# A replanned order, shared PSUM banks, and the bonus term added by VectorE after four SBUF transfers, in a linear-attention and MLP kernel

## The chip, the cores and the metric

The kernel runs on one core of one Trainium2 chip. The metric is the device time of one execution in microseconds (us). One profiled execution gives the trace; its times are counted from the start of its span. TensorE is PE in the profile (PEld is its weight load), VectorE is DVE, ScalarE is ACT, GpSimd is POOL, and SyncE is SP, which issues all DMAs here.

## The reference

The input is `r, k, v, w` of 4 batches, 8 heads, 768 tokens and 48 values a head, and `u` of 8 heads by 48. The attention is a recurrence over the tokens; its output is then, token by token, the input of an MLP.

```python
for t in range(S):
    cur = np.einsum('bhd,bhe->bhde', u[None] * kt, vt)
    y[:, :, t] = np.einsum('bhd,bhde->bhe', rt, state + cur)
    state = wt[:, :, :, None] * state + np.einsum('bhd,bhe->bhde', kt, vt)
...
h = x @ w_in            # x: 3072 x 384, w_in: 384 x 2048
g = np.maximum(h, 0.0) ** 2
return g @ w_out        # w_out: 2048 x 384
```

The part of `y` that comes from `cur` is the bonus: for each token and head one number q, the sum over d of r u k, times the token's v.

## The kernel before, in words

**Tiling.** The 3,072 tokens are 12 steps of 256 tokens; a batch is three steps, and the state S is handed from step to step within it. A step has two chunks (c) of 128 tokens. Loaded tiles hold two neighbouring tokens (j) on one partition, so a partition is a pair of tokens, rows 0 to 63 belong to chunk 0 and rows 64 to 127 to chunk 1. The attention's result y of a step lies in PSUM with other rows: row j x 64 + t and, beside it, the chunk.

**One step of the attention.** `ww_` (L240) multiplies the decays of a pair, `lw_` takes logarithms, `cum_` (L280) sums them by matmuls with triangular matrices, `exp_` and `ac_` (L289, L293) turn the sums into factors, and `rd_` (L301) scales r and k with them. `rw_` and `kw_` (L254, L258) prepare the second row of a pair. The scaled tiles are transposed, in steps 0 to 3 by TensorE (`tr_`, L309, copied out by `rkt_`), and from step 4 by DMA transposes (`dtr_`, L325). `p_` (L330) makes the products of k and r, `pm_` (L344) masks them on VectorE, `su_` (L362) makes the state's update, and `ts_` and `sn_` (L375, L383) apply it on VectorE and GpSimd.

**The bonus.** `ku_` and `qp_` (GpSimd, L262, L267) multiply k, u and r; `q_` (VectorE, L271) sums; `vq_` (GpSimd, L275) multiplies v by it. `vq` has the rows of the loaded tiles. `yq_` (L411) brings it to the rows of y: four matmuls with the 0/1 matrix `spread` add it into y's PSUM tile. `y_` (L399) adds the masked products times v there, and `yc_` (L418) the share of the old state. Helper `y_mm` records all of these, so L394 is the line of `y_`, `yq_` and `yc_` alike; their tiles tell them apart (`v_bf,pmT`, `vq,spread`, `S,rkT`).

**Then the MLP.** `ysb_` (L433) copies y from PSUM to SBUF (ScalarE or VectorE), y is transposed by TensorE (`yt_`, `xt_`) up to step 5 and by DMA (`dyt_`, L451) from step 6. `m1_` (L457) makes an eighth of the first product in six matmuls, `rl_` (L469) applies the ReLU, `sq_` (L477) squares a quarter, `m2_` (L485) makes a quarter of a chunk's second product in four matmuls, `os_` (L492) takes it out of PSUM and `store` writes it.

**What sets the order.** The string ORDER (L17) lists every operation as a word: name, step, part, engine (`=A` ScalarE, `=V` VectorE, `=G` GpSimd) and PSUM bank (`:0`). The last loop records them in that order, and each engine, and SP's one DMA queue, works its words off in it. A planner wrote the string. `pp_` stands for both `p_`, and `yy_` (L426) for the next step's `su_` and the three parts of y.

**PSUM.** Of eight banks, `att0` and `att1` have two each (`cum_`, `p_`, `su_`, `y_`), `bk0` and `bk1` one each (`tr_`, `yt_`, `m2_`) and two more serve `m1_`. SBUF buffers come from pools that rotate.

Of the kernel before, what the change touches and what calls it, by code (L numbers as in the profile page):

```python
# [29 lines left out]
m2_.0.0.1 rl_.1.1=A pm_.2.1 v_.2=G sq_.0.2=A m1_.1.3:0 cast.o.2=G ld.3.v q_.2 m1_.1.6:1 m2_.0.1.0:1 pm_.2.0  # L30
rl_.1.6=A vq_.2 m2_.0.1.1 cast.o.3=A ld.4.w rl_.1.3=V su_.2:0 m2_.0.1.2 ww_.3=G sq_.1.0=A ld.4.r m2_.0.0.2
lw_.3 m2_.0.1.3 sq_.1.1=A cum_.3:1 os_.0.1=V ld.4.k m2_.0.0.3 rw_.3=V exp_.3 m2_.1.0.0:1 ts_.2.0=V kw_.3=G
sq_.1.3=A rd_.3.0 m2_.1.0.1 ld.5.r sn_.2.0 m2_.1.0.2 ac_.3 os_.0.0=A rd_.3.1 m2_.1.0.3 v_.3=A ku_.3
store.0.1 tr_.3.0:0 os_.1.0=V yy_.2:01 ww_.4=V qp_.3 ld.4.v rkt_.3.0=V lw_.4 tr_.3.1:1 ysb_.2=A m2_.1.1.0:0
rkt_.3.1=V ld.5.k ts_.3.0=A cum_.4:1 rw_.4=V sn_.3.0 yt_.2:1 exp_.4 m2_.1.1.1 xt_.2=V ac_.4 ld.5.w m2_.1.1.2
rd_.4.0 kw_.4=G m1_.2.1:1 ts_.3.1=V dtr_.4.0 ku_.4 m1_.2.0:0 rd_.4.1 rl_.2.1=A rl_.2.0=A m1_.2.5:1 q_.3
dtr_.4.1 pp_.3:01 sn_.3.1 rl_.2.5=A m1_.2.3:0 pm_.3.1 ld.6.w vq_.3 m2_.1.1.3 rl_.2.3=A pm_.3.0 m1_.2.2:1
v_.4=A qp_.4 m1_.2.6:0 ld.7.w sq_.2.0=A rl_.2.2=V yy_.3:10 rl_.2.6=V ld.5.v sq_.2.1=A ww_.5=V kw_.5=G
os_.1.1=A m1_.2.4:1 rw_.5=V ld.7.r ysb_.3=A m1_.2.7:0 lw_.5 yt_.3:1 ts_.4.0=V rl_.2.4=A m2_.2.0.0:0 ld.6.k
xt_.3=A sn_.4.0 sq_.2.2=V m2_.2.0.1 ku_.5 cum_.5:0 store.1.1 m2_.2.1.0:1 ac_.5 q_.4 exp_.5 m1_.3.1:1  # L40
ts_.4.1=V rl_.2.7=A m2_.2.1.1 rd_.5.0 rl_.3.1=A m1_.3.7:0 ww_.6=G sq_.2.3=A rd_.5.1 m2_.2.1.2 dtr_.5.0
sn_.4.1 rl_.3.7=A m1_.3.3:1 pp_.4:10 vq_.4 store.0.0 rl_.3.3=A m1_.3.2:0 dtr_.5.1 v_.5=A pm_.4.0 m1_.3.4:1
rl_.3.2=A ww_.7=G pm_.4.1 m2_.2.1.3 ld.6.r lw_.6 rl_.3.4=A qp_.5 m1_.3.0:0 ld.7.k lw_.7 kw_.6=V m2_.2.0.2
sq_.3.1=A ld.6.v yy_.4:10 ku_.6 ld.7.v rl_.3.0=V os_.2.1=V m2_.2.0.3 ysb_.4=A ts_.5.0=V store.1.0 sq_.3.0=V
m1_.3.5:1 sn_.5.0 yt_.4:1 rl_.3.5=A m1_.3.6:0 xt_.4=V sq_.3.2=A ld.8.w pp_.5:10 qp_.6 rl_.3.6=V m1_.4.0:1
os_.2.0=A pm_.5.0 sq_.3.3=A m2_.3.1.0:1 ld.8.r pm_.5.1 m1_.4.5:0 rw_.6=G rl_.4.0=A m2_.3.0.0:0 rw_.7=G q_.5
cum_.6:1 m1_.4.3:1 exp_.6 rl_.4.5=V kw_.7=G m2_.3.1.1 ac_.6 rd_.6.0 rl_.4.3=A cum_.7:0 vq_.5 m1_.4.1:0
exp_.7 rd_.6.1 dtr_.6.0 m2_.3.0.1 ac_.7 rd_.7.0 ww_.8=G v_.6=A m1_.4.2:1 dtr_.6.1 m2_.3.0.2 rd_.7.1
rl_.4.1=A v_.7=G rl_.4.2=A m2_.3.0.3 q_.6 sq_.4.0=A ld.8.k yy_.5:10 vq_.6 sq_.4.1=A m1_.4.4:0 ts_.6.0=A
dtr_.7.0 os_.3.0=A m1_.4.6:1 sn_.6.0 ysb_.5=A m2_.3.1.2 ld.9.r rl_.4.6=V ku_.7 lw_.8 yt_.5:0 store.2.0  # L50
rl_.4.4=A ts_.6.1=V m2_.3.1.3 xt_.5=V ld.9.w pp_.6:01 ld.9.k sn_.6.1 m1_.4.7:1 pm_.6.0 m1_.5.1:0 ku_.8
os_.3.1=V ld.8.v m2_.4.1.0:0 rl_.5.1=A pm_.6.1 dtr_.7.1 m2_.4.1.1 rl_.4.7=A sq_.4.3=A m1_.5.3:0 kw_.8=V
yy_.6:01 rl_.5.3=A ld.11.k sq_.4.2=A m1_.5.0:1 ts_.7.0=V ysb_.6=A m1_.5.4:0 sn_.7.0 rl_.5.0=V dyt_.6
cum_.8:1 rw_.8=G sq_.5.0=A m1_.5.2:1 ld.10.w m2_.4.0.0:1 rl_.5.2=V rl_.5.4=A ww_.9=G m2_.4.0.1 exp_.8
ts_.7.1=V qp_.7 m1_.5.7:0 ac_.8 rd_.8.0 sq_.5.1=A m1_.5.6:1 rd_.8.1 m2_.4.0.2 dtr_.8.0 rw_.9=G m2_.4.0.3
rl_.5.6=V pp_.7:01 q_.7 ld.10.k kw_.9=G os_.4.0=A m1_.5.5:1 lw_.9 dtr_.8.1 pm_.7.1 v_.8=A vq_.7 m2_.5.0.0:1
rl_.5.7=A m2_.5.0.1 store.3.0 pm_.7.0 rl_.5.5=A m1_.6.6:0 ld.9.v sn_.7.1 sq_.5.3=A m1_.6.2:1 rl_.6.6=V qp_.8
yy_.7:10 store.2.1 rl_.6.2=A ld.11.w sq_.5.2=A m1_.6.1:0 ysb_.7=V m1_.6.7:1 rl_.6.1=V dyt_.7 cum_.9:0 q_.8
m2_.4.1.2 exp_.9 m1_.6.5:0 rl_.6.7=A ku_.10 rd_.9.0 m2_.5.0.2 rl_.6.5=A m2_.5.0.3 ts_.8.0=V ac_.9 dtr_.9.0
v_.9=A ww_.10=V m1_.6.0:1 vq_.8 rd_.9.1 m1_.6.4:0 rl_.6.0=A ld.10.r m2_.4.1.3 os_.5.0=V ld.11.r pp_.8:10  # L60
store.3.1 ku_.9 os_.4.1=A m2_.5.1.0:1 sq_.6.3=A pm_.8.1 dtr_.9.1 m1_.6.3:1 rl_.6.4=A sn_.8.0 m2_.5.1.1
sq_.6.0=A rl_.6.3=V store.4.1 m1_.7.7:0 pm_.8.0 store.5.0 m1_.7.0:1 rl_.7.7=A store.4.0 m2_.6.0.0:0 ww_.11=V
ld.10.v kw_.11=V yy_.8:01 lw_.11 rl_.7.0=A rw_.11=V sq_.6.2=A m1_.7.4:0 ts_.9.0=V sq_.6.1=A m2_.5.1.2
sn_.9.0 rl_.7.4=V ysb_.8=A m1_.7.2:1 kw_.10=G lw_.10 ts_.9.1=V m2_.5.1.3 dyt_.8 rl_.7.2=A rw_.10=V m1_.7.1:0
qp_.10 m1_.7.3:1 ld.11.v rl_.7.1=V pp_.9:10 rl_.7.3=A m1_.7.5:0 v_.10=A pm_.9.0 qp_.9 m1_.7.6:1 os_.5.1=A
# [12 lines left out]
rl_.10.1=V dyt_.11 m2_.9.0.0:1 m1_.10.5:1 m2_.9.0.1 rl_.10.5=V m1_.9.6:0 m2_.9.1.1 rl_.9.6=V m1_.10.4:1
m2_.9.1.2 rl_.10.4=A m1_.10.0:0 sq_.10.3=A m1_.11.7:1 rl_.10.0=V m2_.9.0.2 rl_.11.7=V m1_.10.3:0 sq_.9.3=V
m1_.11.3:1 sq_.10.0=V rl_.10.3=A m2_.9.1.3 sq_.10.2=A sq_.10.1=V m1_.11.1:0 rl_.11.3=V os_.9.1=A m2_.9.0.3  # L80
store.9.1 m2_.10.1.0:0 os_.9.0=A m1_.11.0:1 store.9.0 m2_.10.0.0:1 store.8.1 rl_.11.0=A m2_.10.0.1
rl_.11.1=A sq_.11.0=A m2_.10.1.1 m1_.11.4:1 m1_.11.5:0 rl_.11.4=A m2_.10.1.2 rl_.11.5=A m1_.11.2:1
m2_.10.0.2 rl_.11.2=A m2_.10.0.3 sq_.11.1=A m1_.11.6:0 os_.10.0=V sq_.11.2=V m2_.10.1.3 rl_.11.6=A
# [6 lines left out]
def kernel(  # L90
# [54 lines left out]
    def bf16_bank(i):  # L145
        return bk[int(i)][:].bitcast(BF16)
# [420 lines left out]
```

## Time and profile before

| what | value |
|---|---|
| three runs | 188.51, 189.66, 193.23 us (median 189.66) |
| span of the profiled execution | 186.7 us, granted TensorE clock 0.999 |
| the median over that span | 3.0 us |
| busy: PE, DVE, ACT, POOL | 177.0, 125.8, 125.1, 104.9 us |
| m1 matmuls (L464) | 576, 273 ns each |
| m2 matmuls (L489) | 384, 326 ns each |
| bonus matmuls (L394, spread) | 48, 320 ns each |
| `vq` (L277), POOL | 12, 1,520 ns each |
| loads, stores, transposes | 57, 24 and 22, all issued by SP |

The result of the runs holds no time of the profiled execution other than its span. Matmuls are pipelined: each starts before the one ahead has ended, so what one costs is read from start to start, not from its length. A "group" is all instructions of one line, engine and shape. "Idle before" is the time for which an engine stood still ahead of a group, and who ended it.

### The profile page before, as it was taken

What the parts mean: (1) busy time and instruction counts of PE and PEld (TensorE: products, weight loads), DVE (VectorE), ACT (ScalarE), POOL (GpSimd) and SP (SyncE); (2) the same over time, 40 slices, a digit from 0 to 9 for tenths busy, and PEclk for the clock granted to TensorE, in tenths of its full rate; (3) what the DMA queues carried; (4) which work ended last, traced back from release to release, by engine and by line L of the source; (5) the groups of instructions that cost most, each with busy time, mean ns of one, the idle gap of its engine ahead of it and who ended that gap; (6) DMA issues with size and microseconds to landing.
All of it is one profiled execution on the core that took longest, in us unless ns stands there. A gap on an engine that the chain in (4) does not pass through costs nothing.

```text
span 186.7 us, 5422 instructions
## 1 busy us (share of the span) xinstructions
PE 177.0 (95%) x2303; PEld 125.4 (67%) x2303; DVE 125.8 (67%) x170; ACT 125.1 (67%) x205; POOL 104.9 (56%) x99
## 2 busy tenths in 40 slices
PE   7686998999999999999999999999999999999992
PEld 2344587766777777777776766777666777776761
DVE  4379979686799876983849699795946472562020
ACT  5278978889659795797687577968541656156732
POOL 7289627695897998959496981563934130000000
PEclk9999999999999999999999999999999999999999
DMA  6999999999999999979999999890539150203022
GB/s 151 269 274 341 330 280 381 340 280 264 275 234 218 257 239 236 248 148 147 279 185 260 220 270 251 240 147 32 66 63 201 30 172 0 46 0 126 4 84 84
DMA packets 78952, 35.81 MB, mean 192 GB/s; under 512 B 72144, under 2 KB 77392, under 8 KB 78928
## 3 DMA queue, kind: packets, MB, share of 16 engines
q1 hardware_dynamic: 78928, 35.46, 82.5%
q8 instruction: 18, 0.29, 0.7%
q14 instruction: 6, 0.05, 0.1%
HBM read 25.36 MB, written 4.72 MB: 161 GB/s over the span
## 4 chain that ended last, share of the span: by engine, by line
PE 80%; DVE 8%; ACT 5%; issue 3%; DMA 3%; SPq 0%; ACTq 0%
PE m L464 32%; PE bk L489 31%; PE att L394 8%; DVE rdec_buf L305 4%; PE att L341 3%; PE att L371 3%; DMA w_raw<-in_w_dram 3%; PE bk L444 1%; PE att L286 1%; PE att L287 1%; ACT att L291 1%; DVE r_raw L256 1%; ACT ac_buf L298 1%; DVE pmT L351 1%; DVE pmT L354 1%
## 5 line engine op out<-in xcount | busy, mean ns | idle before, releaser
L464 PE MATMUL m<-xT,wi_sb 128*128 128x256 bf16 x576 | 74.3, 273 | 0.5 <-ACT gt L473 0.5
L489 PE MATMUL bk<-wo_sb,gt 128*128 128x384 bf16 x384 | 71.9, 326 | 0.0
L464 PEld LDWEIGHTS <-wi_sb 128*128 128x128 bf16 x576 | 54.9, 98 | 13.9 <-issue 1.4
L473 ACT ACTIVATE gt<-m 128x512 f16<-128x512 f32 x68 | 39.7, 596 | 34.4 <-PE m L464 34.1
L489 PEld LDWEIGHTS <-gt 128*128 128x128 bf16 x384 | 36.9, 98 | 19.3
L481 ACT ACTIVATE gt<-gt 128x1024 bf16<-128x1024 f16 x36 | 37.6, 1053 | 0.9 <-DVE gt L475 0.7
L354 DVE TENSOR_TENSOR pmT<-att,mask 128x1024 bf16<-128x1024 f32 x22 | 26.3, 1218 | 5.6 <-PE att L341 5.5
L386 POOL TENSOR_TENSOR S<-t_state,ac_buf 128x384 bf16<-128x384 f32 x20 | 18.7, 935 | 19.9 <-DVE t_state L381 13.2
L475 DVE TENSOR_SCALAR gt<-m 128x512 f16<-128x512 f32 x28 | 19.2, 687 | 14.6 <-PE m L464 11.9
L264 POOL TENSOR_TENSOR ku<-k_raw,u_bc 128x768 f32<-128x768 f32 x12 | 22.5, 1878 | 9.1 <-DVE q L273 4.7
L269 POOL TENSOR_TENSOR ku<-ku,r_raw 128x768 f32<-128x768 f32 x12 | 22.9, 1910 | 1.0 <-DMA r_raw<-in_r_dram 0.8
L277 POOL TENSOR_TENSOR vq<-v_raw,q 128x768 bf16<-128x768 f32 x12 | 18.2, 1520 | 9.1 <-DVE q L273 4.8
L305 DVE TENSOR_TENSOR rdec_buf<-r_raw,att 128x768 bf16<-128x768 f32 x12 | 11.3, 952 | 3.8 <-ACT att L291 2.2
L498 DVE TENSOR_SCALAR o_sb<-bk 128x384 f32<-128x384 f32 x11 | 6.1, 551 | 11.0 <-PE bk L489 11.0
L291 ACT ACTIVATE att<-att 128x768 f32<-128x768 f32 x12 | 9.4, 795 | 3.7 <-PE att L287 3.6
L305 DVE TENSOR_TENSOR rdec_buf<-k_raw,att 128x768 bf16<-128x768 f32 x12 | 11.4, 947 | 0.5 <-ACT ac_buf L298 0.5
L506 PE MATMUL bk<-warm 128*128 128x512 bf16 x35 | 10.5, 452 | 1.2 <-DVE half_ones L212 1.2
L273 DVE TENSOR_REDUCE q<-ku 128x16 f32<-128x768 f32 x12 | 11.3, 943 | 0.0
L496 ACT ACTIVATE o_sb<-bk 128x384 f32<-128x384 f32 x13 | 6.4, 490 | 6.2 <-PE bk L489 6.2
L483 DVE TENSOR_TENSOR gt<-gt 128x1024 bf16<-128x1024 f16 x12 | 8.9, 753 | 2.0 <-ACT gt L473 2.0
L381 DVE TENSOR_TENSOR t_state<-S,att 128x384 f32<-128x384 bf16 x16 | 8.7, 546 | 1.8 <-PE att L371 1.8
L247 ACT ACTIVATE lw_buf<-ww 128x384 bf16<-128x384 f32 x12 | 6.2, 524 | 5.3 <-DVE ww L243 5.3
(72 smaller groups left out, 179.8 us busy)
## 6 DMA issues: line engine op xcount, KB each, us to landing
w_raw<-in_w_dram SPq DMA_DIRECT2D x12, 384.0 KB, 5.1
k_raw<-in_k_dram SPq DMA_DIRECT2D x12, 384.0 KB, 6.1
r_raw<-in_r_dram SPq DMA_DIRECT2D x12, 384.0 KB, 6.2
v_raw<-in_v_dram SPq DMA_DIRECT2D x12, 384.0 KB, 6.0
out_dram<-o_sb SPq DMA_DIRECT2D x24, 192.0 KB, 3.1
w_st<-in_moe_w_in_dram SPq DMA_DIRECT2D x4, 768.0 KB, 8.5
w_st<-in_moe_w_out_dram SPq DMA_DIRECT2D x4, 768.0 KB, 8.7
rkT<-rdec_buf SPq DMA_TRANSPOSE x16, 4.0
```

The source lines that it names most:

```text
L264: nc.gpsimd.tensor_mul(ku[:], raw["k", s][:, :, 1:3, :], u_bc[:, :, None, :].to_broadcast([C, H, 2, D]))
L269: nc.gpsimd.tensor_mul(ku[:], ku[:], raw["r", s][:, :, 0:2, :])
L277: nc.gpsimd.tensor_mul(vq[:].rearrange("p j h d -> p h j d"), raw["v", s][:], tiles.pop(("q", s))[:, :, :, None].to_broadcast([C, H, 2, D]))
L305: nc.vector.tensor_mul(rdec[:, i, :, :, 0:D], x.rearrange("p h j d -> p j h d"), cs[:, i, 0:DM].rearrange("p (h d) -> p h d", h=H)[:, None ...
L354: nc.vector.tensor_mul(pmT, ps_p[:].rearrange("p e (a x) -> p (e a) x", a=2), mk.to_broadcast([C, 4, 2 * C]))
L386: nc.gpsimd.tensor_mul(t[:], tiles.pop(("ts", s, c))[:].rearrange("p (a e d) -> p a e d", a=HP, e=2), tiles["a_c", s][:, :, c, :, None].to ...
L394: nc.tensor.matmul(ps_y[rows, c, cols], lhsT, rhs, start=fresh, stop=True, skip_group_check=True)
L464: nc.tensor.matmul(ps1[:, j, :], wi_sb[:, n // 4, kk, n % 4 * 128:(n % 4 + 1) * 128], tiles["xT", s][:, :, kk, :], start=(kk == 0), stop=( ...
L473: nc.scalar.activation(rl, m1, AF.Relu, scale=RS)
L475: nc.vector.tensor_scalar(out=rl, in0=m1, scalar1=RS, scalar2=0.0, op0=ALU.mult, op1=ALU.max)
L481: nc.scalar.activation(gt, rl, AF.Square)
L489: nc.tensor.matmul(m2, gt[:, n, c * C:(c + 1) * C], wo_sb[:, n, :], start=(n == 0), stop=(n == NT - 1))
```

## The change

- An SBUF tile `vqt` (two buffers) is new. In steps 2 to 11 (`MOVED`) `yq_` is gone: `mv_` copies `vq` to the rows of y by four DMAs on SP's queue, each of 64 rows of 768 bytes, and `ysb_`, now on VectorE in these steps, adds the copy while it takes y out of PSUM. Steps 0 and 1 keep the matmuls.
- The four single PSUM banks become one set, `one`, that `m1_`, `m2_`, `tr_`, `yt_` and the warming matmuls share; each word names its bank.
- SBUF buffers are taken from lists of free ones in the order of the words, in the numbers of before; `pp_` and `yy_` are gone, and their parts are words of their own.
- ORDER is planned anew. On VectorE there are now 23 squares (before: 12), 35 `rl_` (28), 10 `ysb_` (3), 8 `os_` (11), 2 `xt_` (5), no casts (2), 5 `ww_` (7), 9 `rw_` (8), 7 `kw_` (6); on GpSimd five casts (2), 7 `ww_` (5), 3 `rw_` (4), 5 `kw_` (6).

```diff
+MOVED = range(2, 12)
...
-    bk = [ps_att.tile([C, 512], FP32, name=f"bk{i}") for i in range(2)]
-    m1_bank = [ps_att.tile([C, 512], FP32, name=f"m1_{i}") for i in range(2)]
+    one = [ps_pool.tile([C, 512], FP32, name=f"one{i}") for i in range(4)]
...
+    def buf(kind, *key):
+        held = live.setdefault((kind,) + key, [])
+        if not held:
+            held += [free[kind].pop(0), uses_of(kind, key)]
+        held[1] -= 1
+        if not held[1]:
+            free[kind].append(live.pop((kind,) + key)[0])
+        return held[0]
...
+    def mv_(s):
+        vq, vqt = buf("vq", s), buf("vqt", s)
+        for c in range(2):
+            for j in range(2):
+                nc.sync.dma_start(out=vqt[j * Q:(j + 1) * Q, c, :],
+                                  in_=vq[c * Q:(c + 1) * Q, j].rearrange("p h d -> p (h d)"))
...
     def ysb_(s):
-        y_sb = tiles["ysb", s] = a_mid.tile([C, 2, DM], BF16, name="y_sb")
-        copy = nc.scalar.copy if where["ysb_", s] == "A" else nc.vector.tensor_copy
-        copy(y_sb[:], tiles.pop(("y", s))[:, :, 0:DM])
+        ps_y, y_sb = tiles.pop(("y", s))[:, :, 0:DM], buf("y_sb", s)
+        if s in MOVED:
+            nc.vector.tensor_add(y_sb[:], ps_y, buf("vqt", s)[:])
+        else:
+            (nc.scalar.copy if where["ysb_", s] == "A" else nc.vector.tensor_copy)(y_sb[:], ps_y)
```

The words of the order around the bonus, step 9 before and after (other words between them left out):

```
before: ... q_.9 ... vq_.9 ... yy_.9:01 ... ysb_.9=A ... dyt_.9 ... m1_.9.7:0
after:  ... q_.9 ... vq_.9 ... mv_.9 ... y_.9:1 yc_.9 ... ysb_.9 ... dyt_.9 ... m1_.9.5:0
```

The new order of the first loads is `ld.0.w ld.1.w ld.0.u ld.1.k ld.0.k ld.0.r ld.1.r ld.0.v ld.1.i ld.1.v ld.3.i ld.2.w ld.0.i`; before it was `ld.0.w ld.1.w ld.0.k ld.0.u ld.0.r ld.1.r ld.1.k ld.0.v ld.0.i ld.1.v ld.1.i ld.2.w ld.3.i`. The second product of the first steps comes later than before, and the attention of steps 2 and 3 earlier.

More of the change, by code (lines that the diff above doesn't have):

```diff
@@ L137 @@
-    o_pool = ctx.enter_context(tc.tile_pool(name="moe_out", bufs=4))
-    ps_att = ctx.enter_context(tc.tile_pool(name="ps_att", bufs=1, space=PSUM))
-    att = [ps_att.tile([C, 2, 512], FP32, name=f"att{i}") for i in range(2)]
-    bk = [ps_att.tile([C, 512], FP32, name=f"bk{i}") for i in range(2)]
-    m1_bank = [ps_att.tile([C, 512], FP32, name=f"m1_{i}") for i in range(2)]
-    def bf16_bank(i):
-        return bk[int(i)][:].bitcast(BF16)
-    raw = {}
+    ps_pool = ctx.enter_context(tc.tile_pool(name="psum", bufs=1, space=PSUM))
@@ new lines @@
+    att = [ps_pool.tile([C, 2, 512], FP32, name=f"att{i}") for i in range(2)]
+    one = [ps_pool.tile([C, 512], FP32, name=f"one{i}") for i in range(4)]
+    def bf16_bank(i):
+        return one[i][:].bitcast(BF16)
+    kinds = dict(
+        w=(4, [C, H, 2, D], FP32), r=(4, [C, H, 3, D], FP32), k=(4, [C, H, 3, D], FP32), v=(4, [C, H, 2, D], FP32),
+        w_st=(4, [C, 4 * DM], FP32), ww=(2, [C, H, D], FP32), v_bf=(3, [C, H, 2, D], BF16),
+        ku=(2, [C, H, 2, D], FP32), q=(3, [C, H, 2], FP32), vq=(2, [C, 2, H, D], BF16), vqt=(2, [C, 2, DM], BF16),
+        rkT=(2, [C, 2, 2, HP, C], BF16), pmT=(2, [C, 2, 4, 2, C], BF16), t=(2, [C, DM], FP32),
+        S=(6, [C, HP, 2, D], BF16), y_sb=(2, [C, 2, DM], BF16), xT=(4, [C, 2, KT, C], BF16),
+        gt=(3, [C, NT, T], BF16), o=(4, [C, DM], FP32))
@@ new lines, with uses_of @@
+    free = {kind: [consts.tile(shape, dtype, name=f"{kind}_b{i}") for i in range(n)]
+            for kind, (n, shape, dtype) in kinds.items() if kind != "vqt" or MOVED}
+    uses = dict(w=4, r=4, k=4, v=3, w_st=2, ww=2, v_bf=3, ku=3, q=2, vq=2, vqt=2, rkT=5, pmT=3, t=2, y_sb=2,
+                xT=9, gt=20, o=2)
+    live = {}
+    def uses_of(kind, key):
+        if kind == "S":
+            s, c = key
+            return 2 if c and s % NB == NB - 1 else 3
+        return uses[kind]
+    def buf(kind, *key):
[6 more added lines that the diff above has]
+        return held[0]
@@ L238, with product @@
     tiles = {}
+    def product(name, s):
+        return nc.gpsimd.tensor_mul if where[name, s] == "G" else nc.vector.tensor_mul
     def ww_(s):
-        ww = tiles["ww", s] = a_mid.tile([C, H, D], FP32, name="ww")
-        mul = nc.gpsimd.tensor_mul if where["ww_", s] == "G" else nc.vector.tensor_mul
-        mul(ww[:], raw["w", s][:, :, 0, :], raw["w", s][:, :, 1, :])
+        w_raw = buf("w", s)
+        product("ww_", s)(buf("ww", s)[:], w_raw[:, :, 0, :], w_raw[:, :, 1, :])
     def lw_(s):
@@ L246, in lw_ @@
         lw = tiles["lw", s] = lw_bufs[s % NLW]
-        nc.scalar.activation(lw[:, :, 0:D], tiles.pop(("ww", s))[:], AF.Ln)
+        nc.scalar.activation(lw[:, :, 0:D], buf("ww", s)[:], AF.Ln)
     def v_(s):
-        v_bf = tiles["v", s] = a_mid.tile([C, H, 2, D], BF16, name="v_bf", bufs=3)
         copy = dict(A=nc.scalar.copy, V=nc.vector.tensor_copy, G=nc.gpsimd.tensor_copy)[where["v_", s]]
-        copy(v_bf[:], raw["v", s][:])
+        copy(buf("v_bf", s)[:], buf("v", s)[:])
     def rw_(s):
-        mul = nc.gpsimd.tensor_mul if where["rw_", s] == "G" else nc.vector.tensor_mul
@@ L256, in rw_ @@
[L256 removed]
+        r_raw, w_raw = buf("r", s), buf("w", s)
+        product("rw_", s)(r_raw[:, :, 2, :], r_raw[:, :, 1, :], w_raw[:, :, 0, :])
     def kw_(s):
[L259 to L260 removed]
+        k_raw, w_raw = buf("k", s), buf("w", s)
+        product("kw_", s)(k_raw[:, :, 0, :], k_raw[:, :, 1, :], w_raw[:, :, 1, :])
@@ L314, in tr_, with two_banks @@
                 nc.tensor.transpose(ps_tr[:, j, p, :], rdec[:, i, j, 2 * p:2 * p + 2, :], ident[:])
-    def new_rkt(s, i):
-        if ("rkT", s) not in tiles:
-            tiles["rkT", s] = a_mid.tile([C, 2, 2, HP, C], BF16, name="rkT")
-        return tiles["rkT", s]
     def rkt_(s, i):
         copy = nc.scalar.copy if where["rkt_", s, i] == "A" else nc.vector.tensor_copy
-        copy(new_rkt(s, i)[:, i], tiles.pop(("tr", s, i)))
+        copy(buf("rkT", s)[:, i], tiles.pop(("tr", s, i)))
     def dtr_(s, i):
         nc.sync.dma_start_transpose(
-            out=new_rkt(s, i)[:, i].rearrange("p j a t -> p (j a) t"),
+            out=buf("rkT", s)[:, i].rearrange("p j a t -> p (j a) t"),
             in_=tiles["rdec", s][:, i].rearrange("t j h d -> t (j h d)"))
+    def two_banks(at):
+        return [one[i][:] for i in ((2, 3) if at == "m" else (0, 1))] if at in "mn" else att[int(at)]
     def p_(s, f):
-        rkT = tiles["rkT", s]
-        at = slot["p_", s, f]
-        ps_p = tiles["p", s, f] = [m1_bank[e][:] for e in range(2)] if at == "m" else att[int(at)]
+        rkT = buf("rkT", s)
+        ps_p = tiles["p", s, f] = two_banks(slot["p_", s, f])
         for a in range(2):
@@ L344, in pm_ @@
     def pm_(s, f):
-        if ("pmT", s) not in tiles:
-            tiles["pmT", s] = a_mid.tile([C, 2, 4, 2, C], BF16, name="pmT")
-        pmT, ps_p = tiles["pmT", s][:, f].rearrange("p a j t -> p a (j t)"), tiles.pop(("p", s, f))
+        pmT, ps_p = buf("pmT", s)[:, f].rearrange("p a j t -> p a (j t)"), tiles.pop(("p", s, f))
         mk = mask[:].rearrange("p i j t -> p (i j t)")[:, None, :]
@@ L355, in pm_ @@
                                  mk.to_broadcast([C, 4, 2 * C]))
-    def pp_(s):
-        p_(s, 0)
-        p_(s, 1)
     def su_(s):
-        rdec, v_bf = tiles["rdec", s], tiles["v", s]
-        at = slot["su_", s]
-        ps_su = tiles["su", s] = [m1_bank[c][:] if at == "m" else att[int(at)][:, c, :] for c in range(2)]
+        rdec, v_bf = tiles["rdec", s], buf("v_bf", s)
+        ps_su = tiles["su", s] = [att[int(slot["su_", s])][:, c, :] for c in range(2)]
         n_c = 1 if s % NB == NB - 1 else 2
@@ L400, in y_ @@
         tiles["y", s] = att[int(slot["y_", s])]
-        pmT, v_bf = tiles.pop(("pmT", s)), tiles["v", s]
+        pmT, v_bf = buf("pmT", s), buf("v_bf", s)
         for e in range(2):
@@ L411, in yq_ @@
     def yq_(s):
-        vq = tiles.pop(("vq", s))
+        vq = buf("vq", s)
         for j in range(2):
@@ L477, in sq_ @@
     def sq_(s, q):
-        gt = tiles["gt", s][:, q * 4:(q + 1) * 4, :]
+        gt = buf("gt", s)[:, q * 4:(q + 1) * 4, :]
         rl = gt.bitcast(FP16)
@@ L485, in m2_ @@
     def m2_(s, c, q):
-        gt = tiles["gt", s]
-        m2 = bk[int(slot["m2_", s, c])][:, 0:DM]
+        gt = buf("gt", s)
+        m2 = one[int(slot["m2_", s, c])][:, 0:DM]
         for n in range(4 * q, 4 * q + 4):
@@ L535 @@
             where[(name,) + args] = engine
-            slot.update(zip(takes(name, *args), banks))
+            if bank:
+                slot[(name,) + args[:2]] = bank
             operations[name](*args)
```

251 lines of the change are left out of this document (105 added, 146 removed).

## The prediction

> **What bounds the kernel now.** I read the page first: busy shares and slices.
>
> ```profile
> PE 177.0 (95%) x2303; PEld 125.4 (67%) x2303; DVE 125.8 (67%) x170; ACT 125.1 (67%) x205; POOL 104.9 (56%) x99
> ...
> PE   7686998999999999999999999999999999999992
> ...
> DMA  6999999999999999979999999890539150203022
> ```
>
> TensorE has work from the eighth slice to the last. The DMA engines are full for two thirds of the span, so loads come just in time, but nothing yet says that TensorE waits for them. Its own list of waits answers that:
>
> ```profile
> PE att L284 <- ACT lw_buf L247: 1.4, 1, 1.4
> PE att L394 <- DVE pmT L354: 1.4, 1, 1.4
> PE bk L506 <- DVE half_ones L212: 1.2, 1, 1.2
> PE m L341 <- ACT rkT L323: 1.2, 1, 1.2
> PE m L464 <- ACT gt L473: 0.5, 1, 0.5
> PE att L341 <- DVE rdec_buf L305: 0.4, 1, 0.4
> ```
>
> The first four lie before 20 us. From the first m1 group (23.39 us in the timeline) TensorE hardly waits: what it is given to do sets the end. So the question is what a piece costs in its queue, and the timeline of one step shows it (start, busy, count):
>
> ```profile
> 83.45 0.51 PE L371 MATMUL att<-v_bf,rdec_buf 64*128 64x96 bf16 x16
> 83.80 0.56 PE L394 MATMUL att<-v_bf,pmT 64*128 64x48 bf16 x32
> 84.20 0.48 PE L394 MATMUL att<-vq,spread 64*128 64x384 bf16 x4
> 84.62 0.53 PE L394 MATMUL att<-S,rkT 128*64 128x96 bf16 x16
> 85.08 1.16 PE L464 MATMUL m<-xT,wi_sb 128*128 128x256 bf16 x9
> ```
>
> The four bonus matmuls hold the queue from 84.20 to 84.62, although each lasts 320 ns by its group: two on different rows of the array overlap.
>
> **The change, part by part.** Times below are TensorE's.
>
> Removed: ten groups of four bonus matmuls, 0.42 us each. Start to start, the last one takes 250 ns where a pair takes 163, so some 90 ns of it is the change from half rows to half columns, and that stays between y and yc. 10 x (0.42 - 0.09) = 3.3 us off the path. All other matmuls stay: 96 m1 groups (0.655 us from start to start), 96 m2 groups (0.65), 35 warm ones. Stretches on parts of the array, each costing some 0.1 us to enter and 0.09 to leave, go from 26 to 27: +0.2, about what y gains by standing closer to su and yc.
>
> Moved, the start: I followed the new order by the rows of before. The u load goes up and k of step 1 before k of step 0; with landings 1.4 us apart, k and r are there by 12.6 us. VectorE's chain (L305, L256, L351, L354, L449 at 0.95, 0.55, 1.28, 1.22, 0.55 us) ends with xt of step 0 at 22.9. First m1 group at 22.95 instead of 23.39: -0.4.
>
> Moved, the rest: with no wait at all the old order would need 157.0 us from its first m1 group to TensorE's end (pieces at their usual spacing); it took 159.8, so 2.8 us were waits and bank changes. The new order needs 153.8: 176.8 as its end with no wait. How much waiting comes on top is the open term. I walked all queues by hand to y of step 3, which the new order puts at 51 instead of 56.5: waits of 0.7 us, where the old order had lost 1.5 by then. Beyond, TensorE meets margins under 0.3 us at pm (steps 2, 4, 7) and yt (4, 5), which before had 0.4 or more. Bounds: 0.7 and 6.0 us; I take the old order's 2.8, the nearest measured sum.
>
> Added: ten times four SBUF transfers on SP. Bytes are a store's (192 KB in all), packets of 768 B. The trace's packets last 26 ns at 384 B and 70 ns at 1,536 B; in between 41 ns, 16 of them on each DMA engine: 0.65 us a step (0.42 to 1.12), 6.5 us of queue time. Issuing: stores hold SP 0.33 to 0.58 us when the queue has room, so 1.3 to 2.3 us a step. A lone store lands 1.9 us after its issue, and one behind loads after 5. Nothing of that is on the path as long as the rows are there when yc ends: the order leaves 3.5 to 5 us from vq to the addition at steps 2, 3, 4, 6 and 10, over 6 at the others. What covers it there is TensorE's m1 and m2 work; without it the addition, the transposes and the next m1 are late one to one. SP waits for vq ahead of each; behind it stand raw loads (v of step 3 and four weight loads at step 2, the k loads of steps 4 and 5 at step 3). At step 2 I get vq at 32.8 and the DMA queue nearly empty, a hole of 1 to 1.5 us; the weights then land from 40 and are cast by 41.5, and are first used at 45.3.
>
> Added on VectorE: ten additions from PSUM. Nearest row: L305, same elements, one operand in PSUM, 0.95 us; copies took 0.80 on ScalarE and 0.96 on VectorE. Bounds 0.80 and 1.22 (L354). Also on VectorE: 11 more squares (L483, 0.75), 7 more L475 (0.69), fewer casts, os and xt. Sum +13 us to 139; ScalarE -18 to 107; GpSimd +4 to 109 (three casts at 1.47). All stay under TensorE, hidden by its 154 us. VectorE's densest stretch, TensorE times 60 to 100, goes from 30.5 to 37 us of work in 40.
>
> One thing speaks against so much VectorE work. L483, L243, L256 and L260 read two SBUF tiles; 7 of their 33 instances are drawn out, by 4.9 us together, all beside GpSimd work:
>
> ```profile
> L483 DVE TENSOR_TENSOR gt<-gt x12: 679/683/1146, 25.8 to 177.4; 128x1024 bf16<-128x1024 f16 x12
> ...
> L243 DVE TENSOR_TENSOR ww<-w_raw x7: 548/558/2211, 6.2 to 116.5; 128x384 f32<-128x384 f32 x7
> ```
>
> (The columns are least, median and most ns.) They become 44, so 6.5 us, +1.6. The Trainium skill (SBUF — State Buffer, section "SBUF: two separate sides") says that a VectorE operation with two SBUF inputs and a GpSimd operation that reads SBUF take one port pair in turn, each for its whole instruction. By that rule the drawing out is no accident, and the trace agrees as far as it goes.
>
> Sum: -3.3 (bonus) -0.4 (start) +0.1 (array changes, waits as before) = -3.6. The end is alike: last matmul to end of span 3.5 us in both, one output operation and its store. The profiled span of 186.7 becomes 183.1. The median of the three runs, 189.66, lies 3.0 above that span and the fastest run 1.8; I take the difference off the median: **186.0**.
>
> **The rivals.**
>
> *Fewer waits.* The hand walk holds to the end, 0.7 instead of 2.8: 183.9. For it: slack appears wherever I walked. Against: even the old order, with wider margins, lost 2.8.
>
> *The way from y to the next products becomes the bound.* From yc's end to the first m1, steps 6 to 11, the new order has 4.3, 5.6, 4.6, 4.6, 4.9 and 5.2 us; before it took 5.8 to 9.6. The way needs 0.96 (ysb), then the transpose (L453: 2.7 to 4.8 us to landing, median 3.3), then 0.1: 3.8 to 5.9. With landings as at steps 6 to 8 before (4.84, 4.75, 3.88) the waits are 1.6, 0.3 and 0.4; with 4.8 everywhere 6.2. I price it +3: 189.0. For it: bonus rows and transposes share one queue. Against: from 130 us that queue is nearly idle.
>
> *Drawn-out VectorE instructions.* All 1.6 us of further drawing out lands on the path: 187.6. For it: VectorE at 37 in 40 us. Against: before, at 9.4 of 10 us busy (54 to 64), TensorE did not wait.
>
> *Slower.* The four small transfers each take a store's turn in the DMA queue (landings 0.52 us apart): 2.1 us a step instead of 0.65. Six steps of that lie in the full stretch to 112 us, 12.5 us that push raw loads back, and those had slack of 0 to 3 us mostly (landing to first use). If 9 us of it reach TensorE: 195. It decides from 1.2 us of lateness a step. Against: the queue runs ahead of TensorE later on, with 13 us of TensorE work a step against some 10 of DMA.
>
> **How the numbers follow.** Forecast (waits of 1.8 to 4 us, 185.0 to 187.2) 0.42; fewer waits 0.18; y way 0.20; drawn-out VectorE 0.07; slower 0.13. The range 183.0 to 190.5 holds all but the last and some edges. About 2% (3.8 us) is what a measurement of this kernel can tell from no change. Faster by more: all of fewer waits and 0.22 of the forecast, 0.40; within: 0.47; slower by more: 0.13.
>
> **What would show it.** Right: TensorE's groups without 40 matmuls from spread, y followed by yc in 0.5 us; first m1 near 23.0; TensorE's waits after that a few tenths each; y_sb additions near 0.95 us; the last matmul at 179.6. Wrong: TensorE waiting for xT before m1 (y way), for gt or pmT from VectorE with L483's successor drawn out, or for loads, with SP waiting for vq and raw tiles used the moment they land (slower). The forecast falls if waits after 23 us sum to less than 1.8 or more than 4.

## The result and the profile after

The changed kernel takes 205.45 us (median of 4 runs, 203.80 to 206.09) where the kernel before takes 189.66 (4 runs): a ratio of 1.087, 95% interval 1.080 to 1.093. The forecast was 186.0 with a range to 190.5. It was wrong by 19 us, and in sign.

The page of the changed kernel, busy shares and slices (the span is 204.2 us, 17.5 us longer):

```profile
PE 180.3 (88%) x2263; PEld 127.6 (62%) x2263; DVE 149.4 (73%) x186; ACT 108.3 (53%) x186; POOL 114.4 (56%) x102
...
PE   7946998898699999889988799979989948999992
...
PEclk9996699999999999999999999999999996999999
DMA  6999994199949989989989899889186330320113
```

The 40 matmuls are gone (2263 instead of 2303). But TensorE, full from the eighth slice on before, now has holes in every part of the span. The clock row falls to 6 tenths in two slices of the start and once near the end, and the DMA row has a hole at slices seven and eight. Where TensorE's waits were six lines of 1.4 us and less, they are now spread over all its suppliers (TensorE's list of waits, the longest sums):

```profile
PE one L455 <- DMA xT_b<-y_sb_b: 5.2, 3, 2.5
PE one L323 <- DVE rdec_buf L314: 2.6, 2, 1.7
PE att L347 <- DVE t_b L379: 2.5, 2, 2.1
PE one L455 <- DVE gt_b L464: 1.7, 3, 0.6
```

Laid against the prediction's timetable without waits, TensorE's first m1 group comes at 26.73 us instead of 22.95, and by the last matmul it is 23.6 us late, where the old order had lost 2.8. The second price the prediction quoted, VectorE's squares, is now this (the squares' line in the changed kernel, then the products of r and w; the three numbers are least, median and most ns):

```profile
L472 DVE TENSOR_TENSOR gt_b<-gt_b x23: 679/684/2299, 46.1 to 185.0; 128x1024 bf16<-128x1024 f16 x23
```

```profile
L261 DVE TENSOR_TENSOR r_b<-r_b,w_b x9: 542/1171/1808, 12.6 to 139.2; 128x384 f32<-128x384 f32 x9
```

Of 44 such operations 24 are drawn out, by 17.0 us together; the prediction had put 6.5.

### The profile page after: what moved, and what is told of

The parts are those of the page before. It is cut to its first block, busy times and chain, and to the rows that moved or that the text cites. A ratio compares the mean times of both kernels' runs of the same rounds, so it can differ in the third digit from the quotient of the medians.

```text
span 204.2 us, 5412 instructions
## 1 busy us (share of the span) xinstructions
PE 180.3 (88%) x2263; PEld 127.6 (62%) x2263; DVE 149.4 (73%) x186; ACT 108.3 (53%) x186; POOL 114.4 (56%) x102
## 4 chain that ended last, share of the span: by engine, by line
PE 34%; DVE 13%; DMA 13%; SPq 6%; issue 4%; POOL 3%; ACT 2%; DVEq 0%; POOLq 0%; ACTq 0%
PE one L478 17%; PE one L455 11%; DMA xT_b<-y_sb_b 4%; SPq L286 4%; DVE gt_b L472 3%; DMA vqt_b<-vq_b 3%; DMA w_b<-in_w_dram 3%; PE att L392 3%; DVE rdec_buf L314 3%; DMA v_b<-in_v_dram 2%; DVE y_sb_b L428 2%; POOL vq_b L279 2%; DVE gt_b L464 2%; PE att L347 2%; DVE k_b L265 1%
## 5 line engine op out<-in xcount | busy, mean ns | idle before, releaser
L455 PE MATMUL one<-xT_b,wi_sb 128*128 128x256 bf16 x576 | 72.5, 275 | 7.4 <-DMA xT_b<-y_sb_b 5.2
L478 PE MATMUL one<-wo_sb,gt_b 128*128 128x384 bf16 x384 | 69.7, 326 | 1.1 <-DVE gt_b L472 1.1
L462 ACT ACTIVATE gt_b<-one 128x512 f16<-128x512 f32 x61 | 35.0, 597 | 33.8 <-PE one L455 33.4
L478 PEld LDWEIGHTS <-gt_b 128*128 128x128 bf16 x384 | 36.6, 98 | 22.5 <-DVE gt_b L472 1.4
L464 DVE TENSOR_SCALAR gt_b<-one 128x512 f16<-128x512 f32 x35 | 23.8, 686 | 10.5 <-PE one L455 9.2
L358 DVE TENSOR_TENSOR pmT_b<-att,mask 128x1024 bf16<-128x1024 f32 x22 | 26.3, 1217 | 5.3 <-PE att L347 5.3
L268 POOL TENSOR_TENSOR ku_b<-k_b,u_bc 128x768 f32<-128x768 f32 x12 | 23.3, 1946 | 9.3 <-DMA k_b<-in_k_dram 9.3
L470 ACT ACTIVATE gt_b<-gt_b 128x1024 bf16<-128x1024 f16 x25 | 26.1, 1055 | 4.3 <-DVE gt_b L464 4.3
L273 POOL TENSOR_TENSOR ku_b<-ku_b,r_b 128x768 f32<-128x768 f32 x12 | 23.8, 1988 | 0.2
L472 DVE TENSOR_TENSOR gt_b<-gt_b 128x1024 bf16<-128x1024 f16 x23 | 20.8, 916 | 0.0
```

What stands on the lines that cost most here:

```text
L268: nc.gpsimd.tensor_mul(buf("ku", s)[:], buf("k", s)[:, :, 1:3, :], u_bc[:, :, None, :].to_broadcast([C, H, 2, D]))
L273: nc.gpsimd.tensor_mul(ku[:], ku[:], buf("r", s)[:, :, 0:2, :])
L358: nc.vector.tensor_mul(pmT, ps_p[:].rearrange("p e (a x) -> p (e a) x", a=2), mk.to_broadcast([C, 4, 2 * C]))
L455: nc.tensor.matmul(ps1[:, j, :], wi_sb[:, n // 4, kk, n % 4 * 128:(n % 4 + 1) * 128], xT[:, :, kk, :], start=(kk == 0), stop=(kk == KT - 1))
L462: nc.scalar.activation(rl, m1, AF.Relu, scale=RS)
L464: nc.vector.tensor_scalar(out=rl, in0=m1, scalar1=RS, scalar2=0.0, op0=ALU.mult, op1=ALU.max)
```

## The experiments

Theory Q says that SyncE's queue, held by the transfers, brings the loads late. Theory W (V in the earlier expectations) says that VectorE loses the time beside GpSimd, because of what the new order puts there. C is the clock, S the start, E the new shares of the engines, P (O at first) the order's own thin margins, L the transfer's own lateness. All times are medians; ratios are to runs of the kernel before on the same chip. e3, e6 and e15 to e20 leave out part of what the kernel computes, so they are versions to measure with, not kernels to use.

| run | us | ratio, 95% interval |
|---|---|---|
| changed kernel | 205.45 | 1.087 (1.080 to 1.093) |
| e1: new order, bonus by matmuls | 202.32 | 1.070 (1.064 to 1.077) |
| e2: old order, bonus moved | 205.22 | 1.083 (1.076 to 1.090) |
| e3: changed, transfers do not wait | 205.26 | 1.088 (1.081 to 1.094) |
| e4: changed, start filled | 202.08 | 1.071 (1.065 to 1.077) |
| e5: changed, old engines for squares | 206.09 | 1.091 (1.084 to 1.098) |
| e6: e1, one-input squares | 198.47 | 1.054 (1.050 to 1.059) |
| e7: e1, old start | 202.63 | 1.075 (1.071 to 1.079) |
| e8: e2, GpSimd issues | 210.51 | 1.107 (1.100 to 1.114) |
| e9: e1, old engines | 207.03 | 1.093 (1.090 to 1.096) |
| e11: old order, new engines | 196.47 | 1.043 (1.041 to 1.045) |
| e14: old order, new buffers | 192.53 | 1.021 (1.018 to 1.024) |
| e2b: old order, moved in 9 to 11 | 189.97 | 1.004 (1.002 to 1.007) |
| e15: e1 without products | 190.70 | 1.006 (1.002 to 1.009) |
| e16: changed, without products | 198.00 | 1.042 (1.036 to 1.049) |
| e17: before, without products | 188.38 | 0.993 (0.990 to 0.996) |
| e18: e2 without products | 204.93 | 1.083 (1.077 to 1.090) |
| e19: e14 without products | 187.27 | 0.993 (0.990 to 0.996) |
| e20: e16, transfers do not wait | 196.95 | 1.038 (1.036 to 1.041) |

**The two halves apart.** e1 keeps the new order and undoes the move; e2 keeps the old order and makes it.

```diff
-MOVED = range(2, 12)
+MOVED = range(0)
... ORDER: every mv_ taken out, yq_ put behind y_ in steps 2 to 11
```

> The changed kernel with its order and its banks, but the bonus of steps 2 to 11 added by the four matmuls again, and no transfers. Theory Q (SyncE's queue: the four transfers of a step wait there for the product of v and the bonus and take 2.4 us to issue, so the loads behind them come late): TensorE gets 3.3 us more work, the 3.8 us lost in the start stay, and most of the other 19.8 us of lateness go, so 190 to 195. Theory V (VectorE drawn out beside GpSimd, which the order brings) and theory O (the order itself has thin margins): the lateness stays, 203 to 209.

```diff
 ORDER of before: ... vq_.2 mv_.2 ... vq_.3 mv_.3 ... (steps 2 to 11)
-        yq_(s)
+        if s not in MOVED:
+            yq_(s)
```

> The kernel before, with its own order and banks, and only the bonus of steps 2 to 11 moved: the four transfers of a step are issued by SyncE right behind the word of the product of v and the bonus. Theory Q: the hold is the same in this order, slower than before by 5 us or more, 195 to 205. Theories V and O: the move itself saves the 3.3 us of matmuls less some late rows of y, 186 to 191.

Each half alone costs almost all of it: 13 us for the order without a transfer, 16 us for the move in the old order. They are two causes that do not add up. In the old order both Q and L can be seen: e2's SyncE and then its VectorE at step 3 (start, busy, what):

```profile
58.63 1.85 SPq L330 DMA_TRANSPOSE rkT<-rdec_buf  x1
60.53 0.58 SPq L157 DMA_DIRECT2D w_raw<-in_w_dram  x1
61.21 2.94 SPq L281 DMA_DIRECT2D vqt<-vq  x4
64.19 0.59 SPq L157 DMA_DIRECT2D w_raw<-in_w_dram  x1
```

```profile
67.37 0.96 DVE L442 TENSOR_TENSOR y_sb<-att,vqt 128x768 bf16<-128x768 f32 x1 [2.83 <-DMA vqt<-vq]
```

vq is ready at 60.9 us and y is complete in PSUM at 63.1, but the last of the four transfers lands at 67.2. In front of them SyncE waits for vq (14.8 us over the run, four times), and behind them stand the loads.

**Is it SyncE's wait, the squares, the clock, the start?**

```diff
+    ready = consts.tile([C, 2, H, D], BF16, name="ready")
...
+        nc.gpsimd.memset(ready[:], 0.0)
...
-        vq, vqt = buf("vq", s), buf("vqt", s)
+        buf("vq", s)
+        vq, vqt = ready, buf("vqt", s)
```

> The changed kernel, with the four transfers of each step read from a tile of zeros that is ready from the start instead of the product of v and the bonus. It leaves out the bonus of steps 2 to 11. SyncE no longer waits in front of the transfers (9.8 us on its queue in the profile), but still issues all 40 (24 us). Theory Q, if the wait is what holds the loads: 195 to 199; if the issue time is: 202 to 205. Theories V and O: 204 to 206.

```diff
 ORDER of after, 29 squares on the engine of before (20 to ScalarE, 9 to VectorE), e.g.
-sq_.0.3=V sq_.1.3=V sq_.1.0=V sq_.1.1=V
+sq_.0.3=A sq_.1.3=A sq_.1.0=A sq_.1.1=A
```

> The changed kernel with each square on the engine it had in the kernel before: 12 on VectorE instead of 23, the others on ScalarE. Squares on VectorE are drawn out by 5.3 us in all beside GpSimd. Theory V: faster by 2 to 5 us, 200 to 203. Theories Q and O: nothing, or slower because ScalarE gets 11 more, 205 to 208.

Neither moved the time. In e3 the waits for vq are gone and TensorE is as late as before within 2 us: the wait was covered by the lateness of everything else. In e5 the drawing out on VectorE falls from 17.0 to 10.5 us, but TensorE waits for ScalarE's squares instead (3.2 and 2.3 us): in an order planned for one split, a square on the other engine seems to be late too. Both are misses for the theory that named them.

```diff
 ORDER of after
-warm_.13.2 ... tr_.1.1:1 ... tr_.0.0:3
+warm_.20.2 ... tr_.1.1:1 warm_.4.0 ... tr_.0.0:3 warm_.5.0
```

> The changed kernel with 16 more warm matmuls in the gaps that TensorE has in the start (7 more in the group ahead of the first transposes, 4 and 5 behind two of them), so that its granted clock does not fall to 0.6 at 15 to 25 us. Theory C (the clock that falls after gaps of 1 to 2 us costs the start its time): the first product of the experts starts 1 to 2 us earlier than 26.7 us and the kernel takes 202 to 204. Otherwise, if VectorE's chain sets the start: 205 to 207.

```diff
 e1
-            nc.vector.tensor_mul(gt, rl, rl)
+            nc.vector.tensor_scalar(out=gt, in0=rl, scalar1=RS, scalar2=0.0, op0=ALU.mult, op1=ALU.max)
```

> The replanned order with the bonus by matmuls (202.3 us), and the 23 squares on VectorE replaced by an operation of the same size with one SBUF input (times 16, not below 0). The squares of these quarters are left out of what is computed. Theory V (VectorE's operations with two SBUF inputs are drawn out beside GpSimd's): this takes the 5.3 us of drawing out of VectorE, and more than that of its work, and the time falls by 4 us or more, to 198 or less. If the squares are not what the path waits for: 201 to 203.

```diff
 ORDER of e1, the words ahead of m1_.0.3: as before (cast.i.0 and the loads of w_out later, ld.2.v earlier)
-... ww_.0=V lw_.1 lw_.0 ... kw_.1=V ku_.1 ... kw_.0=V ... rw_.0=V qp_.0
+... ww_.0=V lw_.0 lw_.1 kw_.0=V ... ku_.0 ... rw_.0=V ... qp_.0
```

> The replanned order with the bonus by matmuls (202.3 us), and everything ahead of the first product of the experts in the order of the kernel before (step 0 first, where the new order begins with step 1). Theory S (the start is what the order lost first: 26.6 us instead of 23.4 at the first product): 3 us or more faster, 199 or less. If the margins behind it are so thin that the time is lost again: 200 to 203.

e4 gains 1.6% (3 us): its granted clock is 1.00 instead of 0.975 and the first m1 group comes at 24.61. So C is real and worth about 3 us, and e4 is a better version of the changed kernel, though not of the one before. e7 also starts 1.8 us earlier than e1 and ends no sooner; S is refuted as the main cause. e6 gives 4 us, but its trace shows that the new squares, of 0.42 us undisturbed, are drawn out as well (to 2.05 us), so it made VectorE's work smaller and did not take the drawing out away. Part of its 4 us may also be the clock: its profiled execution had 1.00 throughout, that of e1 0.972.

**The issuing queue, the engines, the buffers, a small dose.**

```diff
 e2
-                nc.sync.dma_start(out=vqt[j * Q:(j + 1) * Q, c, :],
+                nc.gpsimd.dma_start(out=vqt[j * Q:(j + 1) * Q, c, :],
```

> The old order with the bonus moved (205.2 us), with the four transfers of a step issued by GpSimd, which computes what they carry, not by SyncE. Theory Q (SyncE's queue holds the loads and the transposes behind the transfers): 195 or less, unless the issues cost GpSimd more than SyncE. Theory L (the transfer itself is late for y, whoever issues it): 202 to 207.

```diff
 e9: ORDER of e1, 110 words with the engine of before;   e11: ORDER of before, the same 110 with the engine of after
```

> The replanned order with the bonus by matmuls (202.3 us), with each of the 110 operations whose engine the replanning changed put back on its engine of the kernel before; the order of the words is kept. Theory E (the new shares, with more of the work on VectorE, which is drawn out beside GpSimd, are what makes the order slow): most of the 13 us come back, 190 to 195. Theory P (it is the places of the operations in the order, above all of the products and of the step's chain, that leave no margin): 198 to 206.

> The kernel before in its own order, with the 110 operations on the engines that the replanning chose. Theory E: most of the 13 us appear, 198 to 204. Theory P: 188 to 194.

```diff
 e14: functions, buffers and banks of after; ORDER of before (bk0, bk1, m1 banks -> one0 to one3)
```

> The changed kernel's functions, its buffers kept by hand and its four shared banks, run through the order and the engines of the kernel before, with the bonus by matmuls. If the shared banks and buffers cost nothing by themselves: 188 to 190. If they do: 192 or more.

```diff
 e2
-MOVED = range(2, 12)
+MOVED = range(9, 12)
```

> The kernel before, with the bonus moved in steps 9 to 11 alone, where the loads are through and the transfers land 1 us ahead of y (in the run with all ten steps moved: 155.6 against 156.9, 161.9 against 167.0, 177.3 against 177.9). Theory L (a move pays where the transfer lands ahead of y and holds nothing): 3 times 0.33 us less, 187.5 to 188.8 beside about 189. If the issues or the additions cost what the matmuls did: 189 to 190.5.

e8 is worse than e2. Taking the transfers off SyncE does not help, since they still land after y: at step 7 y is complete at 120.8 us and the last transfer lands at 126.6. That speaks for L. It does not exclude Q, because GpSimd, which computes what the transfers carry, now spends 21 us on issuing them (40 of 0.53 us). e9 and e11 both fell outside the ranges named for E and P: the new order is slower with the old engines (207.0 us), and the old order is slower with the new ones (196.5). An order and its split of the work belong together; neither run gives the 13 us to one of them. e2b moves the bonus only where the transfer lands ahead of y: no loss worth the name, but no gain either (+0.4%, in the range named for issues and additions that cost what the matmuls did).

e14 is the surprise that settled it. It runs the same words in the same order as the kernel before and is 2% slower; its first m1 group comes at 25.77 us instead of 23.39. Here is VectorE, then GpSimd, in the kernel before:

```profile
11.93 0.95 DVE L305 TENSOR_TENSOR rdec_buf<-k_raw,att 128x768 bf16<-128x768 f32 x1
12.79 0.55 DVE L256 TENSOR_TENSOR r_raw<-r_raw,w_raw 128x384 f32<-128x384 f32 x1
13.26 0.94 DVE L273 TENSOR_REDUCE q<-ku 128x16 f32<-128x768 f32 x1
```

```profile
10.30 2.10 POOL L269 TENSOR_TENSOR ku<-ku,r_raw 128x768 f32<-128x768 f32 x1
13.20 1.82 POOL L264 TENSOR_TENSOR ku<-k_raw,u_bc 128x768 f32<-128x768 f32 x1 [0.81 <-DMA k_raw<-in_k_dram]
```

And the same two engines in e14:

```profile
11.76 0.95 DVE L315 TENSOR_TENSOR rdec_buf<-k_b,att 128x768 bf16<-128x768 f32 x1
12.63 1.99 DVE L262 TENSOR_TENSOR r_b<-r_b,w_b 128x384 f32<-128x384 f32 x1
14.54 0.94 DVE L277 TENSOR_REDUCE q_b<-ku_b 128x16 f32<-128x768 f32 x1
```

```profile
12.38 1.82 POOL L269 TENSOR_TENSOR ku_b<-k_b,u_bc 128x768 f32<-128x768 f32 x1
14.28 2.01 POOL L274 TENSOR_TENSOR ku_b<-ku_b,r_b 128x768 f32<-128x768 f32 x1
```

With the new buffers the k of step 1 lands 0.8 us *earlier*. GpSimd's product starts at 12.38 instead of 13.20, and VectorE's product of r and w, which had run in 0.55 us in the gap before GpSimd's, now starts under it and takes 1.99: to 14.62, 0.42 us after GpSimd's end at 14.20. The loss then runs down VectorE's chain (the second sum of the bonus starts at 20.50 us instead of 19.23), and the granted clock falls to 0.6 in one slice behind it, which the kernel before does not show.

The product is not slowed, it waits. Over the 12 traces of kernels that keep these products and issue from SyncE, 196 VectorE products and squares started after a GpSimd operation did and more than 0.25 us before its end; 193 of them ended 0.41 to 0.42 us (squares 0.54 to 0.55) after that end, whatever its length. The three others took their usual time: one started beside GpSimd's filling of a tile with zeros (e3), and two within 0.02 us of GpSimd's start (e5, e7). Of the 266 that did not start so, two took over 0.11 us more than their least. The products with an operand in PSUM never waited (the mask of L358: 1208 to 1226 ns over 22).

The Trainium skill (SBUF — State Buffer, section "SBUF: two separate sides") calls the port pair that VectorE and GpSimd share an exclusive lock and no share of bandwidth; "whichever ... starts first gets the pair for the whole instruction". These traces agree, by the constant 0.42 us.

**Without the wait.** If W is the cause, VectorE operations of the same duration that do not wait must give the time back.

```diff
+    def one_input(to, frm):
+        nc.vector.reduce_sum(to, frm[:, :, :, None], axis=AX.X)
...
-        product("rw_", s)(r_raw[:, :, 2, :], r_raw[:, :, 1, :], w_raw[:, :, 0, :])
+        if where["rw_", s] == "G":
+            nc.gpsimd.tensor_mul(r_raw[:, :, 2, :], r_raw[:, :, 1, :], w_raw[:, :, 0, :])
+        else:
+            one_input(r_raw[:, :, 2, :], r_raw[:, :, 1, :])
... the same for kw_ and ww_
-            nc.vector.tensor_mul(gt, rl, rl)
+            with nc.allow_low_precision(reason="one element"):
+                nc.vector.reduce_sum(gt[:, 0:2, :], rl[:, 0:2, :, None], axis=AX.X)
```

> The replanned order with the bonus by matmuls (202.3 us), with VectorE's products of two SBUF tiles (21 of w, r and k, 23 squares) replaced by sums over one element: the same tiles, 384 elements a row for the products, half of each square's 1024, so that each takes about 0.55 and 0.65 us. The products and these squares are left out of what is computed. Such a sum (the sum of the bonus takes 0.94 to 0.95 us in every run) is not expected to wait for GpSimd. Theory W (VectorE's products wait for GpSimd's operation to end, 17 us in this order): 188 to 193. Theory P (the places in the order leave no margin, whatever VectorE takes): 198 or more. In between, the share of each is read off.

> The same edit in the changed kernel (205.5 us, transfers in it). Theory W: 186 to 192, near what the prediction's walk gave with undisturbed durations. If the transfers lose by themselves in this order: 193 to 198, and above e15. Theory P: 200 or more.

> The same edit in the kernel before (188.6 to 189.7 us), whose VectorE waits 4.9 us for GpSimd in 6 of 33 such operations. TensorE waits 2.8 us in all behind its start. Theory W: 0 to 2 us faster, 187 to 189.5. If the edit itself speeds the kernel up (shorter operations, inputs needed earlier): less than 186, and e15 and e16 are to be read against it.

> The same edit in the old order with the bonus moved by SyncE's transfers in all ten steps (205.2 us; VectorE waits 8.7 us for GpSimd there). Theories Q and L (in this order the transfers hold the loads and land after y): 198 to 204. Theory W alone: 192 or less.

The lines of e15 that answer to the two drawn-out ones above (sums in place of the squares, then of the products of r and w):

```profile
L487 DVE TENSOR_REDUCE gt_b<-gt_b x23: 673/676/679, 42.4 to 169.9; 128x512 bf16<-128x512 f16 x23
```

```profile
L246 DVE TENSOR_REDUCE r_b<-r_b x9: 541/544/546, 12.0 to 129.9; 128x384 f32<-128x384 f32 x9
```

and its page:

```profile
PE 178.8 (95%) x2302; PEld 126.9 (67%) x2303; DVE 132.2 (70%) x186; ACT 108.0 (57%) x186; POOL 104.4 (55%) x102
...
PE   7976999999999999999999899999989999999992
```

No operation is drawn out any more, and the new order falls from 202.3 to 190.7 us. GpSimd was held in turn: its busy time falls from 114.0 (e1) to 104.4, and its operations are no longer drawn out either (the product of k and u takes 1.81 to 1.83 us, up to 2.20 in the changed kernel). The kernel before gains 0.7% from the edit, so of the order's 7.0% some 5.8 points (1.070 - 1.006 less 0.007), about 11 us, are the wait, and 1.2 points (2.3 us) are left for the order's margins. One reservation: sums also read fewer tiles than products, so a few may start earlier; e17 is the measure of that, and it is small. That a square's sum writes half of its quarter does not help: the first matmul of each second product reads the half that is written.

e18 does not move at all (204.93 against 205.22): in the old order the transfers cost 16 us by themselves. In the new order without the wait they cost 3.6 points (e16 against e15, 7 us), where the forecast had the move save 3.3 us.

```diff
 e19: e14 with the edit of e15;   e20: e3 with the edit of e15
```

> The old order and engines with the new buffers (192.5 us), with VectorE's products replaced by sums that do not wait for GpSimd, as in the run of the kernel before with that edit (188.4 us). Theory W (the new buffers only shift arrivals, the first k of step 1 lands at 12.3 us and not at 13.1, so that VectorE meets GpSimd's operations): 188 to 189.5. If buffers or shared banks cost something by themselves: 191 or more.

> The changed kernel without VectorE's products (198.0 us), with the transfers reading a tile of zeros that is always there; bonus of steps 2 to 11 and products left out. If SyncE's wait for the product of v and the bonus is what the transfers cost: 189 to 193. If it is the issuing (2.4 us a step on SyncE) and the landing behind the other traffic: 196 to 199.

e19 equals e17: buffers and shared banks cost nothing by themselves; e14's 4 us were the wait and what followed from it. e20 gives 1 us, which its interval does not tell from nothing (1.036 to 1.041 beside 1.036 to 1.049), so SyncE's wait for vq is at most a small part of the transfers' price. In e16 VectorE's additions still wait for the rows in five of the ten steps, and TensorE for the transposes behind them (a line of VectorE's list of waits, then TensorE's timeline):

```profile
DVE y_sb_b L441 <- DMA vqt_b<-vq_b: 8.3, 5, 3.6
```


```profile
160.78 0.94 PE L468 MATMUL one<-xT_b,wi_sb 128*128 128x256 bf16 x7 [2.33 <-DMA xT_b<-y_sb_b]
```

SyncE's timeline at step 10 of e16 shows how the rows come late: the new order has `mv_.11` and two stores ahead of `mv_.10`.

```profile
146.67 2.46 SPq L299 DMA_DIRECT2D vqt_b<-vq_b  x4
149.18 2.10 SPq L504 DMA_DIRECT2D out_dram<-o_b  x2
151.38 2.39 SPq L299 DMA_DIRECT2D vqt_b<-vq_b  x4
156.35 1.22 SPq L458 DMA_TRANSPOSE xT_b<-y_sb_b  x1
```

vq of step 10 is ready at 146.9, y at 152.1, and the last transfer lands at 155.2; then the transpose takes 4.4 us to land (160.7), 2.8 in e15. Over the run the last row lands after y is complete at steps 3, 4, 5, 8 and 10, by 0.5 to 3.1 us, 7.7 us together. In the wait list of e16 TensorE's waits for xT are 5.7 us. The loads come later too: GpSimd waits 29 us for them in e16 and 15 in e15. How the 10 us (3.3 forecast gain, 7 us loss) divide between late rows and late loads was not taken apart; which of the two costs the 16 us of the old order is open as well. No version that computes everything beat the kernel before.

## Why the prediction was wrong, point by point

- **"I take the old order's 2.8"** is the step that failed. The waits behind the start were priced by the old order's sum because it was the nearest measured one, with 6.0 as the upper bound. The runs show 23.6 us of lateness, 3.8 of it in the start. The larger part came from VectorE's products waiting for GpSimd: about 11 of the 13 us that the order costs without a transfer go when they no longer wait (e1, e15). The hand walk that should have borne this out used VectorE's undisturbed durations and stopped at y of step 3.
- **Drawn-out VectorE** was in the text, with its rows and the rule, and was sized as 44/33 of the old sum: 6.5 us in place of 17.0. That scales a count. What counts is how often a product *starts* under a GpSimd operation: 6 of 33 before, 24 of 44 after. The old order has most of them in GpSimd's gaps. The rival's price of 1.6 us should have had its own upper bound: a GpSimd operation takes up to 2.1 us, and each of 44 could meet one. The argument against it (VectorE busy 9.4 of 10 us and TensorE did not wait) spoke of an order in which few of them meet.
- **The start, -0.4**: it was +3.3 against before (26.73, before 23.39). kw of step 0 and rw of steps 0 and 1 took 1.11, 1.08 and 1.18 us in place of 0.55, which is 1.7 us on the chain that the prediction named; the clock that fell to 0.6 in two slices is 2.1 us (26.73 against 24.61 in e4, where the three take the same 1.1 to 1.2 us). Neither was in the sum. With both gone (e16, no such waits and no fall of the clock there) the first m1 group comes at 23.38.
- **The bonus, -3.3**: the 40 matmuls went, and TensorE's queue no longer holds them. No run shows the 3.3 us as time saved: e2b takes out 12 of them, its rows land in time, and its median is no lower, although its profiled execution is 0.8 us shorter from the first m1 group to the last matmul. **The additions at 0.95 us**: right, 0.952 on average.
- **The transfers**: where they follow other traffic they land 0.2 us apart, no store's turn as the slower rival had it. Their issue was just above the upper bounds: 0.59 us each, 2.4 us a step (0.58 and 2.3). "Nothing of that is on the path as long as the rows are there when yc ends" holds, but the rows were not always there: in the changed kernel they land after yc's end at steps 3, 8 and 10, by 1.0, 0.4 and 3.0 us. From vq to the last landing it is 3.8 us at best and 16 at most, and the slack of 3.5 us and more was read from a timetable without waits. The y-way rival had the right wait (xT, 5.2 us where it said 3) and too small a price.
- **The slower rival** had the right sign and only part of the cause. It put all of it on loads pushed back by the transfers; loads do come later with them (GpSimd's 29 us of waiting in e16 beside 15 in e15), but e1, without one transfer, is slow too.

## What to carry to other kernels

Before an order is moved or replanned, list which of VectorE's operations with SBUF operands alone start under a GpSimd operation, and price the new plan by those starts, not by counting operations. The starts are not the whole price: e9 halves the drawing out (8.9 us, 15 starts) and is 5 us slower than e1, with an order that was planned for other engines. A plan tuned without that price is tuned to one timing: in e14 data that came 0.8 us earlier cost 2.4 us of the start. A copy that replaces matmuls pays only if issue, landing and the queue behind it fit between its source and its use with the measured landing times, not the lone ones.

## What the runs showed of the hardware that was not expected

- A VectorE product of SBUF tiles that starts under a GpSimd operation ends a constant 0.42 us (square 0.55) after it; one-element sums (544 and 676 ns, each within 13 ns) and products with a PSUM operand never waited. One-input operations from SBUF to SBUF can wait as well: the squares of e6, 0.42 us undisturbed, ended 0.28 to 0.29 us after GpSimd's operation, and VectorE's casts of the weights (128x1536 f32, 0.96 us), where they started under one, 0.81 to 0.82 us after it.
- In the changed kernel the granted clock fell to 0.6 for two slices although TensorE's longest idle time ahead of them was 1.7 us; with 16 more warm matmuls (e4) it stayed at 1.00. The length of one gap does not decide it: e6, with one of 2.2 us at the same place, kept 1.00 too.
- With the new buffers the first loads landed earlier at the same words: k of step 1 at 12.3 to 12.6 us in e7, e14 and e19, at 13.0 to 13.2 in the seven runs with the buffers of before. The cause is open.
